# Attention and a PReLU MLP in one kernel: other order of MLP units, other first batch, and PReLU split over ACT, DVE and Pool

## The chip, the cores and the metric

One NeuronCore of a Trainium2 chip. The metric is device time of one execution in microseconds (us). The program runs on one core. Engines: PE (TensorE), ACT (ScalarE), DVE (VectorE), POOL (GpSimd), SP (DMA issue).

## The reference

```python
# q, k, v: (8, 12, 448, 64); w_in (768, 2048), w_out (2048, 768), alpha (2048)
q_n, k_n = rmsnorm(q, g_q), rmsnorm(k, g_k)
attn = softmax(q_n @ k_n.T / 8)            # per batch and head
x = (attn @ v) as (3584, 768)
h = x @ w_in
g = np.maximum(h, 0.0) + alpha * np.minimum(h, 0.0)      # PReLU, 0 <= alpha < 0.3
out = g @ w_out
```

## The kernel before: the parts that matter

Attention runs in steps ("gaps", numbered n) of two score tiles each. A pair of heads in both halves (index y, 24 of them) takes 3.5 gaps. Some gaps hold more: the softmax denominators (`den`, D), the product with v (`attv`, A), the transposes of the next q and k (`turn`, T). The MLP of a finished batch is cut into 16 "ups" (one 128-wide slice of h, index ft) and "downs" (one 128-token, 384-wide output), which are dealt out over the gaps to keep PE busy. A period is the ten or eleven gaps of one batch.

```python
psf = tile_pool(name="psf", bufs=2, space=PSUM)     # hT, op and spin share two buffers

def up(b, ft):
    hT = psf.tile([128, 512], FP32, name="hT", tag="mm")
    ...six matmuls...
    ah = ffn.tile([128, S], FP16, name="ah", tag="ah", bufs=3)
    nc.scalar.activation(out=ah, in_=hT[:, :S], func=AF.Copy, scale=alpha_sb[:, ft : ft + 1])
    nc.vector.tensor_max(out=gT[:, ft, ds((b & 1) * S, S)], in0=hT[:, :S], in1=ah)

def down(b0, t, oh):
    op = psf.tile([128, 512], FP32, name="op", tag="mm")
    for ft in range(NF):  nc.tensor.matmul(op, lhsT=gT[:, ft, ts(t, 128)], rhs=w_out_sb[...])
    ...DVE copy to osb, DMA out...

for y in range(G, NG):               # norm of the later q and k, each step in a gap of its own
    n = J * y / 2
    at(n - 12, load_qk, y)
    at(n - 6, square, y, nm)         # Pool
    after(n - 5, reduce, y, nm)      # DVE, 1.04 us each, two of them
    after(n - 4, root, y)            # ACT: Ln, Exp
    at(n - 3, scale, y, nm)          # Pool: qs
```

The softmax here doesn't subtract the row's maximum and nothing guards it: scores larger than these inputs give would overflow.

## Time and profile before

490.0 us (489.69 to 491.02, three runs).

| | before |
|---|---|
| span of the profiled run | 486.5 us |
| PE busy / idle | 448.4 / 38.1 us |
| first up, after its wait for xT (two of its matmuls ran at 51.92) | from 53.25 us |
| PE waits of hT for gT | 17.0 us, 30 waits |
| Pool busy | 166.7 us |

The prediction shows the lines behind this. The page gives for each engine its busy time; a wait is shown as who waited, for whom, the us in total, the number of waits, and the longest.

### The profile page before, as it was taken

The numbers are of one execution on the slowest core, as the hardware profiler recorded it, in microseconds if no ns is written. First come the engines' busy times: TensorE is split into PE (matmuls) and PEld (weight loads), VectorE is DVE, ScalarE is ACT, GpSimd is POOL, SyncE is SP. The second block draws the span as 40 slices with busy tenths as digits, with TensorE's granted clock in tenths as the row PEclk, the third lists the DMA queues.
The fourth block names the chain that finished last, engine by engine and source line by source line (L and its number), as shares of the span: only waits on it lengthen the run. The fifth ranks groups of instructions, "written<-read, shape, count | busy, mean of one in ns | idle before, by whom it ended". The sixth has DMA issues, their size and how long they took to land.

```text
span 486.5 us, 9510 instructions
## 1 busy us (share of the span) xinstructions
PE 448.4 (92%) x4072; PEld 234.3 (48%) x4072; DVE 216.7 (45%) x312; ACT 290.7 (60%) x399; POOL 166.7 (34%) x123
## 2 busy tenths in 40 slices
PE   6768799999999899999999899999999899999995
PEld 2334354544555444554555454554555454454563
DVE  1753545453552454544562444634643542334421
ACT  2688788666754667557765656666776475523300
POOL 2767574606504425405415244423435020000000
PEclk9599999999999999999999999999999999999999
DMA  7999996343605081333532280333511110120122
GB/s 210 158 248 244 239 197 117 71 109 87 134 23 124 20 165 51 91 98 85 96 74 74 70 166 5 105 80 97 100 34 34 34 34 0 34 66 0 34 65 66
DMA packets 32187, 45.46 MB, mean 93 GB/s; under 512 B 5008, under 2 KB 28560, under 8 KB 32144
## 3 DMA queue, kind: packets, MB, share of 16 engines
q1 hardware_dynamic: 19504, 31.67, 25.5%
q0 software_dynamic: 11776, 11.80, 15.3%
q10 hardware_dynamic: 864, 1.38, 1.0%
q8 instruction: 32, 0.52, 0.4%
q14 instruction: 11, 0.09, 0.1%
HBM read 45.62 MB, written 11.01 MB: 116 GB/s over the span
## 4 chain that ended last, share of the span: by engine, by line
PE 71%; DVE 13%; ACT 11%; DMA 2%; issue 2%; POOL 0%; DVEq 0%
PE op L266 31%; PE hT L249 20%; PE sc L189 6%; PE dn L212 6%; DVE ss L133 5%; DVE gT L258 5%; ACT ah L257 5%; PE av L212 5%; ACT expT L201 4%; PE tps L166 3%; DMA nat<-in_q_dram 2%; ACT rden L232 1%; DVE kT L176 1%; DVE qT L174 1%; ACT rden L227 1%
## 5 line engine op out<-in xcount | busy, mean ns | idle before, releaser
L201 ACT ACTIVATE expT<-sc,expb 128x896 f16<-128x896 f32 x168 | 160.2, 1003 | 48.7 <-PE sc L189 48.4
L249 PE MATMUL hT<-xT,w_in_sb 128*128 128x448 f16 x768 | 159.5, 352 | 17.9 <-DVE gT L258 17.0
L266 PE MATMUL op<-w_out_sb,gT 128*128 128x384 f16 x896 | 152.9, 326 | 0.2 <-DVE gT L258 0.2
L150 POOL TENSOR_TENSOR qs<-nat,rr 128x896 f16<-128x896 f32 x45 | 75.0, 1686 | 221.6 <-ACT rr L145 211.8
L257 ACT ACTIVATE ah<-hT,alpha_sb 128x448 f16<-128x448 f32 x128 | 81.1, 634 | 101.7 <-PE hT L249 100.7
L258 DVE TENSOR_TENSOR gT<-hT,ah 128x448 f16<-128x448 f32 x128 | 79.5, 624 | 104.3 <-ACT ah L257 104.2
L249 PEld LDWEIGHTS <-w_in_sb 128*128 128x128 f16 x768 | 72.3, 97 | 95.0 <-issue 35.4
L266 PEld LDWEIGHTS <-gT 128*128 128x128 f16 x896 | 85.0, 98 | 64.1 <-issue 10.5
L276 DVE COPY osb<-op 128x384 f32<-128x384 f32 x56 | 31.2, 558 | 112.1 <-PE op L266 112.1
L127 POOL TENSOR_TENSOR sq<-nat 128x896 f32<-128x896 f32 x44 | 72.9, 1676 | 3.0 <-DVE ss L133 3.0
L189 PE MATMUL sc<-qT,kT 64*64 64x448 f16 x672 | 50.2, 367 | 7.5 <-DVE kT L176 5.8
L133 DVE TENSOR_REDUCE ss<-sq 128x14 f32<-128x896 f32 x48 | 49.7, 1076 | 9.1 <-ACT sq L125 9.1
L240 DVE TENSOR_TENSOR xT<-av,rden 128x896 f16<-128x896 f32 x24 | 26.2, 1091 | 31.6 <-PE av L212 31.6
L212 PE MATMUL av<-expT,vt 64*64 64x448 f16 x672 | 36.0, 349 | 1.2 <-ACT rden L227 1.2
L212 PE MATMUL dn<-expT,ones 64*64 64x448 f16 x672 | 35.9, 349 | 0.0
L189 PEld LDWEIGHTS <-kT 64*64 64x64 f16 x672 | 13.4, 105 | 38.6 <-issue 30.2
L166 PE MATMUL tps<-ident,qs 128*128 128x128 f16 x336 | 24.0, 224 | 4.7 <-POOL qs L150 4.4
L212 PEld LDWEIGHTS <-vt 64*64 64x64 f16 x672 | 20.0, 107 | 13.5 <-issue 2.3
L166 PEld LDWEIGHTS <-qs 128*128 128x128 f16 x336 | 19.4, 100 | 13.5 <-issue 7.0
L212 PEld LDWEIGHTS <-ones 64*64 64x64 f16 x672 | 19.9, 107 | 11.8 <-issue 0.3
L227 ACT ACTIVATE rden<-dn 128x896 f32<-128x896 f32 x24 | 22.0, 916 | 4.8 <-PE dn L212 4.8
L232 ACT ACTIVATE rden<-rden 128x896 f32<-128x896 f32 x24 | 22.7, 947 | 0.3
(25 smaller groups left out, 97.3 us busy)
## 6 DMA issues: line engine op xcount, KB each, us to landing
out_dram<-osb SPq DMA_DIRECT2D x56, 192.0 KB, 2.7
nat<-in_q_dram SPq DMA_DIRECT2D x45, 224.0 KB, 3.8
nat<-in_k_dram SPq DMA_DIRECT2D x45, 224.0 KB, 5.0
vt<-in_v_dram POOLq DMA_DIRECT2D x16, 336.0 KB, 6.5
w_in_sb<-in_moe_w_in_dram POOLq DMA_DIRECT2D x4, 768.0 KB, 19.4
w_out_sb<-in_moe_w_out_dram POOLq DMA_DIRECT2D x4, 768.0 KB, 14.6
nat<-in_q_dram ACTq DMA_DIRECT2D x3, 224.0 KB, 6.9
nat<-in_k_dram ACTq DMA_DIRECT2D x3, 224.0 KB, 5.9
```

What stands on the lines that cost most here:

```text
L127: nc.gpsimd.tensor_mul(out=sqf, in0=src, in1=src)
L133: nc.vector.tensor_reduce(out=ss_t[y][:, "qk".index(nm)].rearrange("p h j -> p (h j)").unsqueeze(2), in_=sqs[y, nm], axis=AXIS_X, op=ALU.add,)
L150: eng.tensor_mul(out=t.rearrange("p j h d -> p h j d"), in0=nat[y, nm], in1=rr_t[y][:, "qk".index(nm)].unsqueeze(3).broadcast_to((128, 2, ...
L166: nc.tensor.transpose(tp[:, j, :], qs[y, nm][:, j].rearrange("p h d -> p (h d)"), ident)
L189: nc.tensor.matmul(out=sc[ds(64 * g, 64), par, :S], lhsT=kT[ds(64 * par, 64), g, j, :], rhs=qT[ds(64 * par, 64), g].rearrange("p j c -> p ...
L201: nc.scalar.activation(out=expT[y][:, j], in_=scs[y, j][:, :, :S], func=AF.Exp, scale=QK_SCALE, bias=expb[:, 0:1],)
L212: nc.tensor.matmul(out=acc[ds(64 * par, 64), g, :S], lhsT=weights(g, par, j), rhs=e[ds(64 * g, 64), j, par, :], start=(j == 0), stop=(j == ...
L249: nc.tensor.matmul(out=hT[:, :S], lhsT=w_in_sb[:, c, ts(ft, 128)], rhs=x[:, c, :], start=(c == 0), stop=(c == KM - 1),)
L257: nc.scalar.activation(out=ah, in_=hT[:, :S], func=AF.Copy, scale=alpha_sb[:, ft : ft + 1])
L258: nc.vector.tensor_max(out=gT[:, ft, ds((b & 1) * S, S)], in0=hT[:, :S], in1=ah)
L266: nc.tensor.matmul(out=op[:, :OH], lhsT=gT[:, ft, ts(t, 128)], rhs=w_out_sb[:, ft, ds(oh * OH, OH)], start=(ft == 0), stop=(ft == NF - 1),)
L276: nc.vector.tensor_copy(out=o[:, ds(oh * OH, OH)], in_=op[:, :OH])
```

## The change

Its intent: empty the PSUM buffer of an up faster (ACT and DVE read it side by side, Pool adds), put downs where DVE is busy with something else and reductions under downs, and start the first batch sooner. The diff, cut to its core:

```diff
@@ load_qk
-                (nc.scalar if y < G and g else nc.sync).dma_start(
+                (nc.scalar if y < 2 and g else nc.sync).dma_start(
@@ up
-        ah = ffn.tile([128, S], FP16, name="ah", tag="ah", bufs=3)
-        nc.scalar.activation(out=ah, in_=hT[:, :S], func=AF.Copy, scale=alpha_sb[:, ft : ft + 1])
-        nc.vector.tensor_max(out=gT[...], in0=hT[:, :S], in1=ah)
+        pos = ffn.tile([128, S], FP16, name="pos", tag="pos", bufs=4)
+        nc.scalar.activation(out=pos, in_=hT[:, :S], func=AF.Relu)
+        neg = ffn.tile([128, S], FP16, name="neg", tag="neg", bufs=4)
+        nc.vector.tensor_scalar(out=neg, in0=hT[:, :S], scalar1=0.0,
+            scalar2=alpha_sb[:, ft : ft + 1], op0=ALU.min, op1=ALU.mult)
+        nc.gpsimd.tensor_add(out=gT[...], in0=pos, in1=neg)
@@ down: jobs (the reductions) stand between its matmuls and its copy
+        for f, a in jobs:
+            f(*a)
@@ norm of later pairs
-        n = J * y / 2
-        at(n - 12, load_qk, y)   ... square n - 6, reduce n - 5, root n - 4, scale n - 3
+        n = turn_at[y - 1] if y < G + 2 else last(y - G) + 2
+        at(n - 8, load_qk, y)    ... square n - 2, reduce n (under the down of gap n), root and scale n + 1
@@ deal of units over gaps
-        ups and old downs merged evenly, then the new downs
+        in gaps with A or T: an old down first; else ups first; then the new downs
-        tail = len(new) if b == B - 1 else len(new) // 2
+        tail = len(new) if b == B - 1 else 2 + odd
@@ first batch
-    spin(32)                     +    spin(34)
-        after(1, reduce, 2, nm)  +        after(2, reduce, 2, nm)
-    after(2, root, 2)            +    roots[3] = 2     # root, scale after the exponentials
```

More of the change, by code (lines that the diff above doesn't have):

```diff
@@ L255, in up, with down @@
             )
-        ah = ffn.tile([128, S], FP16, name="ah", tag="ah", bufs=3)
-        nc.scalar.activation(out=ah, in_=hT[:, :S], func=AF.Copy, scale=alpha_sb[:, ft : ft + 1])
-        nc.vector.tensor_max(out=gT[:, ft, ds((b & 1) * S, S)], in0=hT[:, :S], in1=ah)
+        pos = ffn.tile([128, S], FP16, name="pos", tag="pos", bufs=4)
+        nc.scalar.activation(out=pos, in_=hT[:, :S], func=AF.Relu)
+        neg = ffn.tile([128, S], FP16, name="neg", tag="neg", bufs=4)
+        nc.vector.tensor_scalar(
+            out=neg, in0=hT[:, :S], scalar1=0.0, scalar2=alpha_sb[:, ft : ft + 1],
+            op0=ALU.min, op1=ALU.mult,
+        )
+        nc.gpsimd.tensor_add(out=gT[:, ft, ds((b & 1) * S, S)], in0=pos, in1=neg)
     osb = {}
-    def down(b0, t, oh):
+    def down(b0, t, oh, jobs=()):
         op = psf.tile([128, 512], FP32, name="op", tag="mm")
@@ L300 @@
     avs = {last(y) + 2: y for y in range(NG)}
-    prep, post = {}, {}
+    prep, post, roots = {}, {}, {}
     def at(n, f, *a):
@@ L307, in after @@
         post.setdefault(max(int(n), 0), []).append((f, a))
+    turn_at = [J * y // 2 - 1 for y in range(NG)]
+    turns = {n: y for y, n in enumerate(turn_at) if y}
+    jobs = {}
     for y in range(G, NG):
-        n = J * y / 2
-        at(n - 12, load_qk, y)
+        n = turn_at[y - 1] if y < G + 2 else last(y - G) + 2
+        at(n - 8, load_qk, y)
         for nm in "qk":
-            at(n - 6, square, y, nm)
-            after(n - 5, reduce, y, nm)
-        after(n - 4, root, y)
-        for nm in "qk":
-            at(n - 3, scale, y, nm)
+            at(n - 2, square, y, nm)
+            if y < G + 2:
+                after(n, reduce, y, nm)
+            else:
+                jobs.setdefault(n, []).append((reduce, (y, nm)))
+        roots[n + 1] = y
     for b in range(1, B):
         at(J * G * b / 2 - 4, load_v, b)
-    turns = {J * y // 2 - 1: y for y in range(1, NG)}
     UP, DOWN = 1.13, 2.6
-    def merge(ups, downs):
-        res, done = [], 0
-        for n, u in enumerate(ups):
-            while done < len(downs) and done * len(ups) <= n * len(downs):
-                res.append(downs[done])
-                done += 1
-            res.append(u)
-        return res + downs[done:]
     periods, carry = [], []
@@ L341 @@
         ]
-        tail = len(new) if b == B - 1 else len(new) // 2
-        periods.append(merge(ups, carry) + new[:tail])
+        tail = len(new) if b == B - 1 else 2 + odd
+        periods.append((ups, carry, new[:tail]))
         carry = new[tail:]
@@ L353 @@
         hi = last(G * b + 2 * G - 1) + 2
-        mlp = sum(u[0] for u in periods[b])
+        ups, old, new = (list(u) for u in periods[b])
+        mlp = sum(u[0] for u in ups + old + new)
         per = (mlp + sum(cost(n) for n in range(lo, hi))) / (hi - lo)
-        n, clock, done = lo, cost(lo), 0.0
-        for u in periods[b]:
-            while n < hi - 1 and clock + 0.5 * u[0] > per * (n - lo + 1):
-                n += 1
-                clock += cost(n)
-            gaps[n].append(u[1:])
-            clock += u[0]
-    rest = [u[1:] for u in periods[B - 1]]
+        clock = 0.0
+        for n in range(lo, hi):
+            clock += cost(n)
+            free = n in avs or n in turns
+            while ups or old or new:
+                if old and (free or not ups):
+                    u = old.pop(0)
+                elif ups:
+                    u = ups.pop(0)
+                else:
+                    u = new.pop(0)
+                gaps[n].append(u[1:])
+                clock += u[0]
+                free = False
+                ahead = 0.5 * (UP if ups else DOWN)
+                if n < hi - 1 and clock + ahead > per * (n - lo + 1):
+                    break
+    ups, old, new = periods[B - 1]
+    rest = []
+    for n, u in enumerate(ups):
+        if n % 3 == 0 and old:
+            rest.append(old.pop(0)[1:])
+        rest.append(u[1:])
+    rest += [u[1:] for u in old + new]
     load_qk(0)
@@ L373 @@
     nc.sync.dma_start(out=alpha_sb, in_=moe_alpha.rearrange("(t p) -> p t", p=128))
-    spin(32)
+    spin(34)
     for nm in "qk":
@@ L395 @@
         after(0, scale, 1, nm)
-        after(1, reduce, 2, nm)
-    after(2, root, 2)
-    for nm in "qk":
-        after(2, scale, 2, nm)
+        after(2, reduce, 2, nm)
+    roots[3] = 2
     for n in range(NB + 2):
@@ L406 @@
             score(*t)
-        late = []
         if n in dens:
@@ L413 @@
         wait = plain and gaps[n] and gaps[n][0][0] is up
+        late = []
         for t in tiles[:1] if wait else tiles:
@@ L416 @@
         if wait:
-            late = [(soft, t) for t in tiles[1:]]
+            late = [(1, soft, t) for t in tiles[1:]]
         if n in dens:
             log(dens[n])
-            late = [(invert, (dens[n],))]
+            late = [(2, invert, (dens[n],))]
+        if n in roots:
+            y = roots[n]
+            root(y)
+            for nm in "qk":
+                scale(y, nm)
         if n in turns:
             turn(turns[n])
+        done = 0
         for f, a in gaps[n]:
-            f(*a)
-            if f is up and late:
-                for g, c in late:
-                    g(*c)
-                late = []
-        for g, c in late:
+            if f is down:
+                down(*a, jobs.pop(n, ()))
+            else:
+                f(*a)
+                done += 1
+                if late and done == late[0][0]:
+                    for _, g, c in late:
+                        g(*c)
+                    late = []
+        for _, g, c in late:
             g(*c)
         if n < first:
-            spin(1 if not plain else 4)
-        for f, a in post.get(n, ()):
+            spin(4 if plain else 1)
+        for f, a in jobs.pop(n, []) + post.get(n, []):
             f(*a)
```

## The prediction

> **What bounds the kernel now.** I read the page's busy shares first, then the waits of the PE alone, then tables by window, then the PE and DVE timelines of one period in the middle (182 to 241 us).
>
> ```profile
> PE 448.4 (92%) x4072; PEld 234.3 (48%) x4072; DVE 216.7 (45%) x312; ACT 290.7 (60%) x399; POOL 166.7 (34%) x123
> ...
> PE hT L249 <- DVE gT L258: 17.0, 30, 1.4
> PE sc L189 <- DVE kT L176: 5.8, 4, 2.0
> PE tps L166 <- POOL qs L150: 4.4, 1, 4.4
> ```
>
> PE is the bound: 448.4 of 486.5 us. All that can be won is its idle 38 us. Of this, 17.0 us in 30 waits is an up-projection (hT) waiting until the PSUM buffer of the unit two before is emptied: hT, op and spin share two buffers, and a unit is free when ACT (ah) and then DVE (gT) have read it. The rest lies in the first 53 us and at the very end.
>
> ```profile
> 0.00:20.00 20.00, 12.86 (x66) 5.72 (x66) 7.48 (x12) 8.12 (x13) 7.92 (x15) 0.80 0.83 185
> 20.00:40.00 20.00, 14.67 (x193) 7.07 (x189) 10.56 (x11) 16.87 (x23) 16.31 (x14) 0.95 1.13 231
> 40.00:60.00 20.00, 15.86 (x183) 8.16 (x183) 10.01 (x13) 16.67 (x21) 11.69 (x9) 1.00 1.17 244
> ...
> 182.00:240.00 58.00, 55.38 (x522) 29.16 (x524) 29.31 (x42) 37.46 (x55) 22.78 (x16) 1.00 0.35 81
> ```
>
> The columns are PE, PEld, DVE, ACT and POOL busy us. From 20 to 53 us there is attention alone (spin matmuls pad PE), and ACT with its exponentials is the fullest engine, some 16.8 of 20 us. Later PE is busy 55.4 of 58 us: a period loses only 2.6 us.
>
> ```profile
> 218.88 2.07 DVE L133 TENSOR_REDUCE ss<-sq 128x14 f32<-128x896 f32 x2
> 220.87 1.26 DVE L258 TENSOR_TENSOR gT<-hT,ah 128x448 f16<-128x448 f32 x2
> ...
> 221.53 1.29 PE L249 MATMUL hT<-xT,w_in_sb 128*128 128x448 f16 x6 [1.02 <-DVE gT L258]
> 216.34 1.30 PE L249 MATMUL hT<-xT,w_in_sb 128*128 128x448 f16 x6 [0.25 <-DVE gT L258]
> ```
>
> This is what a wait consists of. A third up in a row waits 0.25 us by the chain ACT 0.63 + DVE 0.62 + hand-overs, less the 1.15 us of the up between. Where the two 1.04 us reductions stand in DVE's queue ahead of gT, it is 1.02 us (1.36 with other work beside). So the large waits come from where the reductions are put.
>
> **What the Trainium skill says.** (1) "PSUM — Partial Sum Buffer", section "PSUM bank collisions raise a hardware error": two engines may not touch one bank and partition quadrant together, ScalarE read beside VectorE read included, so software orders them. Relu "beside" alpha*min is therefore not beside it. In the built order of the changed program each DVE neg waits for ACT alone and not for PE: it follows pos on the same hT. The trace of before can't show this, as its gT needed ah anyway. (2) "ScalarE: Activation LUTs", section "What ACT_TABLE_LOAD costs": an ACTIVATE takes 186 ns + 0.833 ns per element, and 93 ns more per pointer operand. For 448 elements with one pointer that is 652 ns; the trace's ah takes 634, so it agrees. Relu has no pointer: estimate 634 - 93 = 541 ns. (3) "GPSIMD Engine Reference", section 3.1: a two-input add of 2048 fp32 took 4497 ns, 2.2 ns per element. The trace is faster, 1686 ns for 896 (1.88), so I use the trace. (4) "VectorE: DVE Perf Modes", the perf-mode tier table: two-input and one-input operations with an fp32 PSUM source both run at 1x. So neg should take what gT took, 0.62 us.
>
> **The change part by part.**
>
> PReLU. The chain that frees a PSUM buffer goes from 0.63 + 0.62 to an estimated 0.54 + 0.62 us. The back-to-back wait falls from 0.25 to about 0.16. ACT saves 128 x 0.09 = 12 us of busy time, which is hidden later on. Pool gets 128 adds at 448 x 1.88 ns = 0.84 us (estimate), 108 us: 166.7 + 108 = 274 us, 56% of the span, not a bound. But gT is now ready a Pool add later, and Pool is a queue in order.
>
> Reductions and order of units. The reductions of a pair of heads move to the gap after the attention-value product, between the down-projection's matmuls (2.65 us on PE) and its copy, and there they are hidden. A down goes first where DVE is busy with xT or with qT and kT. This should remove the eight or so 1.02 to 1.36 us waits. But in gaps that have no down they still stand in DVE's queue, now ahead of qT and kT of the next gap, whose scores then wait.
>
> I walked through both kinds of period with the trace's durations (scores 0.41, den or av 1.43, transposes 0.79, up 1.17, down 2.65, exp 0.89, log 0.82, root 0.55, reduction 1.04, qT and kT together 1.2, qs 1.68).
> - Even period: two gaps of three ups after den 0.24 each; five ups in a row 0.4; up, up, down at the end of the period 0.35 for the buffer. Then the down's weights ft 14 and 15 come from the last two ups, whose adds stand on Pool behind two qs of 3.35 us that wait for root. Gap-local: root ends at 2.8, qs at 6.1, the adds at 7.0 and 7.9. The down starts at 3.95 and wants ft 14 at 3.95 + 14 x 0.164 = 6.25, so it stalls 0.8 + 0.75, some 1.5 us. Sum 2.75.
> - Odd period: small waits 0.75 in sum; at its end three ups with no down, reductions behind them, then two ups beside the turn: kT late by 0.75, buffer 0.35, and the same Pool stall 1.5. Sum 3.35.
> - Before, a pair of periods lost 4.57 us (0.24, 1.36, 0.34, 1.02, 0.25, 1.02, 0.34 in the PE timeline). After: 6.1.
> - First period of the MLP: reductions at the end of gaps without a down, kT late three times, 3.8 us against 3.2. Last period with attention 0.75, as no qs is left. The tail of ups and downs 1.5 against 1.8.
> Sum after: 3.8 + 3 x 3.35 + 2 x 2.75 + 0.75 + 1.5 = 21.6 us, against 17.0 + 0.8 (the first up's wait for xT) = 17.8 before. The middle loses 3.8 us.
>
> First batch. Before, ACT itself issues the loads of the third pair, which wait for earlier transfers: the issue at 8.68 keeps it from squaring until 9.33 us, while q of the first pair had landed near 4.9. After, q is squared near 5.0 and k at its landing (8.65), not at 10.2. The k chain (reduction, Ln, Exp, DVE scale, transposes) then gives first scores some 1.5 us earlier, and near 2.0 with PE's pause shortened from 4.4 to about 2 us, since the granted clock at 12 to 18 us was 0.50 and may now stay up. From then on ACT leads. Reductions behind qT and kT and root behind the exponentials remove the 2.04 us wait for kT and some 0.95 us of ACT idle, while one new ACT wait for reductions (0.9) comes at the fourth gap. Gap by gap the lead goes 2.3, 2.5, 3.6, 3.1. The head wins 3.1 us.
>
> Sum: 490.0 + 3.8 - 3.1 = 490.7. The walk leaves no slack for hand-overs that happen to overlap, and its stalls are upper sides, while a saved wait is sure where the reductions lie under a down. I take 1.7 us off for this and predict 489.0.
>
> **Rivals.**
> (a) ACT and DVE do run side by side, or the Pool stall is absent because the last adds get ahead of qs. Then the middle loses only the small waits: some 21.6 - 7.5 (five stalls of 1.5) = 14 us, with the head 490 - 3.7 - 3.1 = 483; without the late kT as well 480. For it: Pool is idle over 60% before. Against it: the built order has qs ahead of those adds, and neg behind pos.
> (b) Pool becomes a moving bound: an add takes 1.2 us or more (the skill's two-input rate plus a fixed part), so pos and neg, four buffers each, run out, and ACT waits for Pool. Each period then loses 2 to 3 us more: 505. For it: rough Pool times. Against it: 16 adds and three pairs of sq and qs take 13.4 + 20.2 = 34 us of a 58 us period.
> (c) The head's gain is hidden: the weights or the loads of later pairs set the first up. Then 493. Against it: w_in is issued at 21.3 and lands within some 20 us, before 53.
>
> **Range and chances.** The base case is 489; (a) in part draws to 481, (c) and longer stalls to 496. Range 481 to 496. Faster by over 2% needs under 480.2, all of (a): 0.12. Slower by over 2% needs (b), over 499.8: 0.07. Within 2%: 0.81.
>
> **What would show it.** Right: first exponential near 15.3 us rather than 17.6; first up near 50; pos near 540 ns, neg near 620 with its idle time ended by ACT pos; Pool adds near 0.84 us; the 1.0 to 1.4 us waits of hT gone, with waits of hT near 0.2; new waits of PE (its weight loads) for Pool gT at the ends of periods, about 1.5 us each, and of scores for kT of about 0.75. PE idle in the middle 2.5 to 3.5 us a period. Wrong: neg running at the same time as pos; no waits for Pool gT; many ACT waits for Pool; a first exponential no earlier than before.

## The result, and the profile after

495.5 us (494.99 to 496.0, four runs) against 490.5 (489.69 to 491.06). The ratio is 1.0103, 95% interval 1.0082 to 1.0124: 1% slower. A second run of the changed kernel later gave 1.0115.

The page's busy line and the waits of PE alone, changed kernel:

```profile
PE 453.5 (92%) x4074; PEld 234.8 (48%) x4074; DVE 224.5 (45%) x312; ACT 277.4 (56%) x399; POOL 296.1 (60%) x251
...
PE hT L249 <- DVE neg L260: 8.5, 25, 1.1
PE sc L189 <- DVE kT L176: 7.4, 10, 1.3
PE op L272 <- POOL gT L264: 7.4, 10, 0.8
PE sc L189 <- ACT expT L201: 3.9, 7, 1.0
```

The waits of hT were halved, 17.0 to 8.5 us. A new wait of the downs for Pool, 7.4 us, and more waits of scores came in their place. The three groups of PReLU (busy us, mean ns; then idle time ahead of them and what ended it):

```profile
L264 POOL TENSOR_TENSOR gT<-pos,neg 128x448 f16<-128x448 f16 x128 | 130.1, 1030 | 105.9 <-DVE neg L260 102.7
L260 DVE TENSOR_SCALAR neg<-hT,alpha_sb 128x448 f16<-128x448 f32 x128 | 86.9, 684 | 120.9 <-ACT pos L258 120.9
L258 ACT ACTIVATE pos<-hT 128x448 f16<-128x448 f32 x128 | 68.7, 543 | 110.7 <-PE hT L249 104.8
```

All of neg's 120.9 us of idle time was ended by ACT's pos: the two readers of one hT run one after the other, 0.54 + 0.68 us, where before it was 0.63 + 0.62. Next to nothing was gained on the chain, 1.23 against 1.26 us. The windows by stage, to be read as those in the prediction:

```profile
0.00:20.00 20.00, 15.77 (x76) 6.36 (x80) 9.52 (x14) 10.03 (x15) 10.20 (x17) 0.85 0.96 200
...
182.00:240.00 58.00, 54.73 (x530) 28.53 (x529) 27.36 (x38) 34.43 (x51) 37.20 (x32) 1.00 0.30 67
```

The middle is a little emptier on PE (54.73 of 58 us, 55.38 before). To see where the 7.0 us of span arise, I compared the start of the logarithm of each pair of heads (ACT, line 227, one per pair) in both timelines:

| pair y | before | after | after - before |
|---|---|---|---|
| 2 (end of the head) | 49.50 | 47.29 | -2.21 |
| 8 | 149.59 | 148.51 | -1.08 |
| 14 | 261.37 | 263.81 | +2.44 |
| 20 | 373.13 | 379.10 | +5.97 |
| 23 | 427.55 | 431.92 | +4.37 |
| end of span | 486.5 | 493.5 | +7.0 |

The head wins 2.2 us. Two periods (y = 8 to 14) take 115.30 us in place of 111.78, so 1.8 us are lost in each. From y = 23 to the end 2.6 us more pass; one down (2.65 us on PE) has moved from the periods to the end, and what it costs there was saved earlier. From the end of the head to the end of the span the changed kernel therefore loses 7.0 + 2.2 = 9.2 us; this is the middle of the prediction.

The end of period 1 shows the main loss. Lines of the timeline of the changed kernel (start, us, engine, operation; in brackets the idle time before, and what ended it):

```profile
137.88 0.96 ACT L258 ACTIVATE pos<-hT 128x448 f16<-128x448 f32 x2
138.05 3.33 POOL L150 TENSOR_TENSOR qs<-nat,rr 128x896 f16<-128x896 f32 x2 [1.56 <-ACT rr L145]
138.44 1.28 DVE L260 TENSOR_SCALAR neg<-hT,alpha_sb 128x448 f16<-128x448 f32 x2
...
139.18 2.44 PE L272 MATMUL op<-w_out_sb,gT 128*128 128x384 f16 x14 [0.25 <-DVE neg L260]
...
141.34 2.01 POOL L264 TENSOR_TENSOR gT<-pos,neg 128x448 f16<-128x448 f16 x2
...
142.43 0.34 PE L272 MATMUL op<-w_out_sb,gT 128*128 128x384 f16 x1 [0.82 <-POOL gT L264]
...
143.41 2.77 PE L272 MATMUL op<-w_out_sb,gT 128*128 128x384 f16 x16 [0.65 <-POOL gT L264]
```

pos and neg of the last two ups are done at 139.7. Pool is in two qs until 141.4 and adds them only then. The down does 14 matmuls and stops for ft 14 and again for ft 15. Its 16th matmul starts 4.23 us after its first, where 15 x 0.1625 = 2.44 us is normal (16 matmuls take 2.60 us when nothing stops them): 1.79 us lost. The recorded waits are 1.47 us, less than that, since the record of a matmul that stands alone (0.34 us) is longer than its place in a full stream (0.16). The same stall appears at 202, 257, 317 and 373 us.

### The profile page after: what moved, and what is told of

The parts are those of the page before. It is cut to its first block, busy times and chain, and to the rows that moved or that the text cites. A ratio compares the mean times of both kernels' runs of the same rounds, so it can differ in the third digit from the quotient of the medians.

```text
span 493.5 us, 9659 instructions
## 1 busy us (share of the span) xinstructions
PE 453.5 (92%) x4074; PEld 234.8 (48%) x4074; DVE 224.5 (45%) x312; ACT 277.4 (56%) x399; POOL 296.1 (60%) x251
## 3 DMA queue, kind: packets, MB, share of 16 engines
q0 software_dynamic: 11776, 11.80, 15.3%
## 4 chain that ended last, share of the span: by engine, by line
PE 61%; POOL 13%; ACT 9%; DVE 8%; issue 6%; DMA 1%; POOLq 0%; SPq 0%; ACTq 0%; DVEq 0%
PE op L272 26%; PE hT L249 17%; PE sc L189 6%; PE av L212 6%; POOL qs L150 5%; PE dn L212 4%; DVE neg L260 4%; POOL sq L127 4%; ACT pos L258 4%; POOL gT L264 3%; ACT expT L201 3%; DVE ss L133 3%; PE tps L166 2%; DMA nat<-in_k_dram 1%; POOL vt L102 1%
## 5 line engine op out<-in xcount | busy, mean ns | idle before, releaser
L264 POOL TENSOR_TENSOR gT<-pos,neg 128x448 f16<-128x448 f16 x128 | 130.1, 1030 | 105.9 <-DVE neg L260 102.7
L272 PE MATMUL op<-w_out_sb,gT 128*128 128x384 f16 x896 | 155.3, 327 | 9.0 <-POOL gT L264 7.4
L260 DVE TENSOR_SCALAR neg<-hT,alpha_sb 128x448 f16<-128x448 f32 x128 | 86.9, 684 | 120.9 <-ACT pos L258 120.9
L258 ACT ACTIVATE pos<-hT 128x448 f16<-128x448 f32 x128 | 68.7, 543 | 110.7 <-PE hT L249 104.8
L272 PEld LDWEIGHTS <-gT 128*128 128x128 f16 x896 | 84.9, 98 | 74.3 <-POOL gT L264 11.2
L150 POOL TENSOR_TENSOR qs<-nat,rr 128x896 f16<-128x896 f32 x45 | 75.0, 1688 | 58.0 <-ACT rr L145 46.9
L284 DVE COPY osb<-op 128x384 f32<-128x384 f32 x56 | 31.1, 555 | 95.6 <-PE op L272 95.6
L189 PE MATMUL sc<-qT,kT 64*64 64x448 f16 x672 | 51.7, 370 | 11.4 <-DVE kT L176 7.4
```

Of the source, the lines that this page charges most:

```text
L150: eng.tensor_mul(out=t.rearrange("p j h d -> p h j d"), in0=nat[y, nm], in1=rr_t[y][:, "qk".index(nm)].unsqueeze(3).broadcast_to((128, 2, ...
L189: nc.tensor.matmul(out=sc[ds(64 * g, 64), par, :S], lhsT=kT[ds(64 * par, 64), g, j, :], rhs=qT[ds(64 * par, 64), g].rearrange("p j c -> p ...
L258: nc.scalar.activation(out=pos, in_=hT[:, :S], func=AF.Relu)
L260: nc.vector.tensor_scalar(out=neg, in0=hT[:, :S], scalar1=0.0, scalar2=alpha_sb[:, ft : ft + 1], op0=ALU.min, op1=ALU.mult,)
L264: nc.gpsimd.tensor_add(out=gT[:, ft, ds((b & 1) * S, S)], in0=pos, in1=neg)
L272: nc.tensor.matmul(out=op[:, :OH], lhsT=gT[:, ft, ts(t, 128)], rhs=w_out_sb[:, ft, ds(oh * OH, OH)], start=(ft == 0), stop=(ft == NF - 1),)
```

## The experiments

All were correct. Each was timed with three rounds against the kernel before on the same chip; the kernel before had medians of 488.54 (first four), 489.58 (next four) and 489.66 us (last two), so the differences, and not the times, are to be compared across chips.

| run | median us | against before, us | ratio (95%) |
|---|---|---|---|
| changed kernel | 495.48 | +5.0 | 1.0103 (1.0082 to 1.0124) |
| r1_old_prelu | 482.35 | -6.2 | 0.9878 (0.9849 to 0.9907) |
| r2_only_prelu | 494.54 | +6.0 | 1.0123 (1.0098 to 1.0148) |
| r3_head_only | 486.47 | -2.1 | 0.9951 (0.9920 to 0.9982) |
| r4_last_two | 484.19 | -4.4 | 0.9909 (0.9883 to 0.9934) |
| r5_add_on_dve | 490.25 | +0.7 | 1.0014 (0.9980 to 1.0049) |
| r6_old_prelu_late_red | 479.25 | -10.3 | 0.9792 (0.9759 to 0.9825) |
| r7_eight_bufs | 492.24 | +2.7 | 1.0057 (1.0023 to 1.0091) |
| r8_late_red | 486.64 | -2.9 | 0.9941 (0.9902 to 0.9981) |
| r9_early_red | 477.87 | -11.8 | 0.9766 (0.9747 to 0.9785) |
| r10_after_again | 495.01 | +5.4 | 1.0115 (1.0091 to 1.0138) |

**r1_old_prelu: everything but the PReLU.**

```diff
 changed kernel
-        pos = ...Relu;  neg = ...min, mult;  nc.gpsimd.tensor_add(out=gT[...], in0=pos, in1=neg)
+        ah = ...Copy, scale=alpha;  nc.vector.tensor_max(out=gT[...], in0=hT[:, :S], in1=ah)
```

> The changed kernel with the PReLU of before (ACT copy times alpha, DVE max); gap order and first batch as changed. Theory (the loss sits in the Pool add: five stalls of 1.8 us at the ends of periods 1 to 5, counted from the first down's start to its 16th matmul, a buffer stall of some 1.5 us near 83 us, and a DVE part of 0.68 instead of 0.62 us): 485 us, that is 10 below the changed kernel, and no PE wait for Pool gT. Rival (the new order of units and the reductions placed behind ups without a down cost it): 494 us, as the PReLU would not matter.

6.2 us below before and 11.2 below the changed kernel (-6.2 against +5.0), and no wait for Pool gT is left among PE's. The rival falls: order and first batch are good by themselves. In r1's profiled run 0.84 us comes from an early landing of k; see the head in the part on the prediction. PE's waits in this run:

```profile
PE hT L249 <- DVE gT L259: 6.5, 25, 0.3
PE sc L189 <- DVE kT L176: 4.5, 5, 1.3
PE sc L189 <- ACT expT L201: 3.5, 7, 0.5
PE sc L189 <- ACT ah L258: 2.9, 5, 0.8
```

The longest wait of hT is 0.3 us, where it was 1.4 before: the reductions are out of its way.

r1 and the changed kernel have the same order, so their logarithms can be compared pair by pair. The lead of r1 grows in steps and is nearly flat in between:

| pair y at which the lead grows | step, us | what is there in the changed kernel |
|---|---|---|
| 8, 14, 20 | 1.87 each | stall of the down, odd periods |
| 11, 17 | 1.78, 1.77 | stall of the down, even periods |
| 5 | 1.56 | ACT waits 2.19 us for Pool gT at 81 us |
| 10, 16 | 0.89, 0.88 | ACT waits 1.70 and 1.69 us for Pool gT at 185 and 301 us |
| 3 to 23, in sum | 12.2 | five stalls 9.2 and three buffer waits 3.3, less 0.3 of drift |

**r2_only_prelu: the PReLU alone.** The same edit the other way round, on the kernel before.

> The kernel before with only the PReLU of the change. If the PReLU is dear by itself, as a longer chain with a Pool step: 498 us or more. Theory: it is dear only where a down follows the last ups and qs stands ahead of their adds on Pool; in the order of before the qs are issued gaps later, so the adds are done in time and the kernel takes 491 to 493 us (0.03 us more in each short wait, a few waits of ACT for the four buffers).

6.0 us slower. The theory had 491 to 493 us, some 1 to 3 above the 490 of the kernel before, and the rival 498 or more: neither size is right. Between pairs 4 and 5 the distance to the kernel before changes from -0.9 to +5.1 us, and by only 0.5 us in all the pairs after that, though ACT waits 17.4 us in this run for Pool's work (14.4 of them recorded as for qs): nearly all of that is hidden. So the PReLU is not dear by itself, but in one place. The timeline there, and then the kernel before at the same place:

```profile
80.75 3.33 POOL L150 TENSOR_TENSOR qs<-nat,rr 128x896 f16<-128x896 f32 x2
84.04 3.31 POOL L127 TENSOR_TENSOR sq<-nat 128x896 f32<-128x896 f32 x2
87.32 2.01 POOL L263 TENSOR_TENSOR gT<-pos,neg 128x448 f16<-128x448 f16 x2
...
88.39 0.34 PE L271 MATMUL op<-w_out_sb,gT 128*128 128x384 f16 x1 [1.96 <-POOL gT L263]
89.38 0.50 PE L271 MATMUL op<-w_out_sb,gT 128*128 128x384 f16 x1 [0.65 <-POOL gT L263]
...
92.17 4.48 PE L271 MATMUL op<-w_out_sb,gT 128*128 128x384 f16 x16
```

```profile
84.83 2.77 PE L266 MATMUL op<-w_out_sb,gT 128*128 128x384 f16 x16
87.54 0.57 PE L189 MATMUL sc<-qT,kT 64*64 64x448 f16 x8
```

It is the same mechanism in one place: two adds behind 6.6 us of qs and sq. And two things cost time. The first down takes 5.83 us to the next scores (2.71 in the kernel before at the same place), so 3.1 us are the stall. Then the granted clock has fallen: the columns of the windows are as before, the clock is third from the end.

```profile
88.00:90.00 2.00, 0.95 (x6) 0.39 (x10) 0.08 (x1) 0.00 (x0) 1.33 (x2) 0.70 0.02 3
90.00:92.00 2.00, 2.00 (x21) 1.30 (x14) 2.00 (x3) 1.55 (x2) 0.00 (x0) 0.50 0.00 0
```

At half clock the stretch from these scores to the next ones takes 6.77 us in place of 3.99, which is the other 2.8 us. That the pause of PE brought the clock down is read from the order in this one trace, and no run tests it.

**r3_head_only: the first batch alone.** The kernel before with the loads of the third pair off ACT's queue, `spin(34)`, and reductions and roots of pairs 2 to 4 placed as in the change.

> The kernel before with only the first batch reordered (loads of the third pair off ACT's queue, reductions behind qT and kT, root behind the exponentials, for the pairs 0 to 4). Theory: the first up starts 2.2 us earlier, as in the changed kernel, and nothing takes it back: 488.3 us. Rival (the gain in the head is hidden by a later wait): 490.3.

2.1 us faster by the medians, 2.4 by the ratio. In its profiled run the lead of 1.9 us at pair 2 stands unchanged at pair 23: nothing takes it back.

**r4_last_two: Pool adds for 14 of 16 slices only.**

```diff
 changed kernel, up()
+        if ft >= NF - 2:
+            ...ah and tensor_max of the kernel before...
+            return
         pos = ...
```

> The changed kernel, but the last two ups of each batch (ft 14 and 15) with the PReLU of before, so only 16 of 128 adds leave Pool. Theory (the five stalls of the first down behind qs are the main loss): 495.5 - 5 x 1.8 = 486.5 us and no PE wait for Pool gT at ft 14 and 15. Rival (Pool's load as a whole, or the chain of ACT and DVE, costs it): 494 us, an eighth of the difference.

9.4 us below the changed kernel with only 16 of 128 adds taken from Pool. The rival, that Pool's load or the chain costs it, would have given one eighth. Pair by pair r4 gains five steps of 1.78 to 1.82 us where the stalls were, 9.0 in sum, and a sixth of 1.53 us near 83 us, as it also takes the first of the three buffer waits away; the other two stay. In this run qs still stands on Pool at that place, and the down runs through (the row goes on past the 16 matmuls of one down):

```profile
137.17 4.06 PE L277 MATMUL op<-w_out_sb,gT 128*128 128x384 f16 x24 [0.28 <-DVE gT L260]
...
136.02 3.33 POOL L150 TENSOR_TENSOR qs<-nat,rr 128x896 f16<-128x896 f32 x2 [1.56 <-ACT rr L145]
```

**r5_add_on_dve: the add on DVE.**

```diff
-        nc.gpsimd.tensor_add(out=gT[...], in0=pos, in1=neg)
+        nc.vector.tensor_add(out=gT[...], in0=pos, in1=neg)
```

> The changed kernel with the sum of pos and neg on DVE instead of Pool; Relu on ACT and alpha*min on DVE stay. Theory (Pool's queue delays gT; the split itself costs only 0.03 us per short wait): no PE wait for gT longer than 0.3 us, and 1 to 2 us above the kernel with the whole PReLU of before, that is about 5 us below the kernel before. Rival (three instructions in place of two are what costs): above the kernel before, as DVE now has one more instruction on the chain.

+0.7 us (the interval of the ratio takes in 1), where I expected about -5: a miss. There is no wait for Pool's gT, but hT now waits up to 0.7 us. The add on DVE took 560 ns in the mean, and 128 of them stand in the queue that also frees hT:

```profile
L264 DVE TENSOR_TENSOR gT<-pos,neg 128x448 f16<-128x448 f16 x128 | 71.7, 560 | 4.4
...
PE hT L249 <- DVE neg L260: 11.1, 31, 0.7
PE sc L189 <- DVE kT L176: 9.9, 10, 1.3
```

The mean hides two kinds. By tile, the 128 adds last 391 ns at the least, 393 in the middle and 1577 at the most. The 93 during which Pool ran nothing took 391 to 394 ns each; the 32 that met a square (sq) or a qs there took 600 to 1577, and 3 that met only the issue of a load took 392 or 393. The views by tile, of Pool and of DVE:

```profile
L264 DVE TENSOR_TENSOR gT<-pos,neg x128: 391/393/1577, 52.6 to 463.1; 128x448 f16<-128x448 f16 x128
103.34 3.46 POOL L127 TENSOR_TENSOR sq<-nat 128x896 f32<-128x896 f32 x2
103.69 1.57 DVE L264 TENSOR_TENSOR gT<-pos,neg 128x448 f16<-128x448 f16 x1
```

So the add left Pool's queue, but was still slow whenever one of Pool's long operations ran. neg beside it (670 to 686 ns) and the gT of the kernel before (614 to 626) show nothing of the kind. This is read from the trace; no run without Pool's work at those places tests it. The split into three instructions is dear on DVE too: the PReLU of two instructions is 6.9 us better in the same order (r1).

**r7_eight_bufs: pos and neg with eight buffers.**

```diff
-  pos ... bufs=4    neg ... bufs=4
+  pos ... bufs=8    neg ... bufs=8
```

> The changed kernel with eight buffers in place of four for pos and neg. Theory (Pool's backlog reaches ACT only near 78 to 84 us, where ACT waits for Pool gT 5.6 us in three waits and scores follow by 1.5 us): at most 2 us below the changed kernel, the stalls of the downs unchanged. Rival (the backlog is general): 5 us or more.

2.3 us below the changed kernel (2.7 against r10), about the 2 us expected. The place was read wrongly: the three waits are not all near 78 to 84 us, but at 81, 185 and 301 us. At all three Pool has a pair of squares (3.3 us) and the issue of a load of v (1.35 us) ahead of the adds. Pair by pair r7 gains 1.59, 0.86 and 0.85 us there, 3.3 in sum, and nothing elsewhere. ACT's waits for Pool go from 5.6 to 0.4 us, and the waits of hT of 1.1 us go. The stalls of the downs stay: PE's waits for Pool gT read 7.4 us in ten here too. Changed kernel (sum of the waits, and one of the three in the timeline), then this run:

```profile
ACT pos L258 <- POOL gT L264: 5.6, 3, 2.2
185.22 0.54 ACT L258 ACTIVATE pos<-hT 128x448 f16<-128x448 f32 x1 [1.70 <-POOL gT L264]
```

```profile
ACT pos L258 <- POOL gT L264: 0.4, 2, 0.2
```

**r8_late_red: reductions, root and qs of pairs 10, 16, 22 two gaps later.**

```diff
 changed kernel, norm of later pairs
         n = turn_at[y - 1] if y < G + 2 else last(y - G) + 2
+        if y in (10, 16, 22):
+            n += 2
```

> The changed kernel, PReLU with Pool kept, with the reductions, root and qs of the pairs 10, 16 and 22 two gaps later. So at the end of the odd periods qs stands behind the adds of the last two ups and not ahead of them. Theory: the stalls for Pool gT of periods 1, 3 and 5 go (3 x 1.8 us), and the kT wait with them (3 x 0.8): 7 to 8 us below the changed kernel, 2 to 3 below the kernel before; those of periods 2 and 4 stay. Rival (the adds are late by their own load on Pool, not by qs): stalls stay in all five, 2 to 3 us gained.

2.9 us below before, 7.9 below the changed kernel, as expected. PReLU and the number of adds are the same. The whole preparation of three pairs (loads, squares, reductions, root, qs) comes two gaps later, so the order on Pool is not all that changes. The stalls fall from five to two:

```profile
PE op L272 <- POOL gT L264: 3.0, 4, 0.8
PE sc L189 <- DVE kT L176: 5.8, 7, 1.3
```

How much of the gain is the stalls? r6, below, makes the same shift without adds on Pool. Pair by pair it gains 1.05 us on r1 at each of y = 8, 14 and 20; r8 gains 2.86 us on the changed kernel at each. The difference, 1.81 us each or 5.4 in sum, is one stall each (by the medians, across chips, the sum is 3.8). So it is the place of qs ahead of the adds, and not the load of the adds.

**r6_old_prelu_late_red and r9_early_red: towards a version that beats both.** r6 is r1 with the edit of r8. r9 is r6 with one more:

```diff
+        if y in (5, 6, 7):
+            n -= 1
```

> The changed kernel with the PReLU of before, and the reductions of the pairs 10, 16 and 22 (the ones that stand behind three ups in a gap without a down) two gaps later, under a down. Theory: this takes away kT late by 0.55 to 0.8 and a buffer wait of 0.25 to 0.3 with their refill, three times: some 3 us below r1_old_prelu, 9 us below the kernel before. Rival (the scores' wait for kT hides another wait just behind it): the same as r1_old_prelu, 6 us below.

> r6_old_prelu_late_red with the reductions of the pairs 5, 6 and 7 one gap earlier, so that they stand ahead of the attention-value product and not ahead of the next qT and kT. Theory: the three waits of scores for kT between 57 and 89 us (0.8, 0.55, 0.4 us in the changed kernel) and their followers go: 2 us below r6_old_prelu_late_red, 12 below the kernel before. Rival (xT behind the reductions becomes the wait): no gain, 10 below the kernel before.

r6 came out 10.3 us below before, 4.1 below r1 by the differences. r9 came out 11.8 below, the expected 12, and 1.5 below r6; across chips, that last step is about as small as the noise, but in the traces it lies where it was expected: r9's lead over r6 grows by 1.96 us between pairs 2 and 4. r9 is the best kernel, 477.87 us. Its PE waits:

```profile
PE hT L249 <- DVE gT L259: 6.2, 24, 0.3
PE sc L189 <- DVE kT L176: 4.0, 4, 1.3
PE sc L189 <- ACT expT L201: 2.4, 5, 0.5
```

The four kT waits that are left all lie in the head (before 50 us); hT waits only the short 0.3 us of a third up in a row.

**r10_after_again: the changed kernel beside r9.**

> The changed kernel itself once more, on the chip and in the rounds of r9_early_red, so that the two are compared directly: 1.0% above the kernel before, as in its first run, by both theories; r9_early_red then 16 to 17 us below it.

495.01 against 477.87 us on one chip in the same rounds, 17.1 us apart.

## Why the prediction was right or wrong

489.0 was predicted, 481 to 496 as range, within 2% with a chance of 0.81. Measured were 495.5 us and +1.0%: within 2% and just inside the range, but on the other side of 490 from the point. The steps:

- **ACT and DVE do not read hT side by side: right.** All of neg's idle time ends with pos. pos took 543 ns (541 predicted).
- **The Pool stall at the ends of periods 1 to 5, through qs ahead of the last two adds: right in place, number and recorded size.** 10 waits in five pairs, 7.4 us in sum, 1.5 each predicted and recorded. r4, and r8 beside r6, show its cause.
- **The new order of units: right in size.** Without its 7.5 us of stalls the walk gives 14.1 us against 17.8, a gain of 3.7 in the middle. r1, which has the order without the Pool adds, gains 3.35 there in its trace.
- **Durations: two were too short.** The Pool add was scaled in proportion, 0.84 us, and took 1.03. neg was taken as equal to gT, 0.62, and took 0.68; the short wait of hT became 0.28 and not 0.16 us, of which neg explains 0.06. It mattered little: r1's 25 waits of hT sum to 6.5 us, those of r7 with the new PReLU to 6.9.
- **The sum of the middle: 3.8 us predicted, 9.2 found. This is the step that failed in size.** Two terms make up 5.0 of the missing 5.4 us. A stall costs some 1.8 us of PE's time and not its recorded 1.5: 9.2 in place of 7.5 (table in r1). And four buffers did run out: ACT waited for Pool three times, which costs 3.3 us in the traces (r7; 2.3 to 2.7 by the medians). This I had named as rival (b) and put aside by comparing Pool's busy time with the period. Pool is busy only 60%, but its work comes in blocks of 3.3 us. The order's missing 0.35 us is the rest.
- **The head: 3.1 us predicted, 2.2 found.** The start was right: the first exponential is at 15.38 us (15.3 predicted, 17.64 before), q is squared at 5.06 and k at 8.70. The lead predicted from there, 3.1, was 2.66 at the exponentials ahead of pair 0's logarithm and 2.21 at pair 2. Between the two the transposes wait 0.51 us for Pool's qs at 41.19, whose root now comes later, and ACT then waits 0.77 us for scores; the kernel before does not wait there. The clock did not stay up, as I had hoped: it was granted 0.50 between 14 and 20 us. But that cost nothing at pair 2. r1, with the clock at 1.00 there, and r5 have the same head and are at -3.05 and -2.91; they squared k at 7.84 and 7.99 us, and this 0.86 and 0.71 us is all of their lead over the changed kernel (0.84 and 0.70). r3, r4 and r10 fit this within 0.02 us, so the head of a run shifts with the landing of k; r6 to r9 lose 0.3 to 0.5 us more ahead of pair 2, which was not traced.
- **The 1.7 us taken off at the end: wrong in direction.** I read my walk as an upper side. It was a lower one, as every unexpected size made a wait longer.
- Rival (a) fell with neg's waits and the 7.4 us of waits for Pool, rival (c) with r3. Rival (b) came true in three places.

That the result lies inside the range, by half a us, is partly luck. The range ended at 496 for rival (c) and longer stalls. The stalls were longer by only 0.3 us each and (c) did not come, but part of (b), which the range left out, took its place.

Where did the expected gain of the change go? Order and first batch together are worth 6.2 us (r1), of which the first batch is 2.1 to 2.4 (r3). The new PReLU costs 11.2 us on top by the medians, 12.2 in the traces between pairs 2 and 23: 9.2 in five stalls of downs and 3.3 in three waits for buffers (r4 takes away 9.0 of the first and 1.5 of the second, r7 the 3.3).

Left open: why the DVE add of r5 is slow beside Pool's long operations, whether PE's pause brought the clock down in r2, and why neg takes 0.06 us longer than gT did.

## What to carry to other kernels

Before work is moved to an idle engine, look at what stands ahead of it in that engine's queue and who needs its result next: here an engine that was 34% busy, in blocks of 3.3 us, held up 1 us adds by 1.6 us (at 141 us) and, in r2, by 3.2. The split across two engines that read the same PSUM tile bought no overlap; look at what the second reader waits for in the built program. And a mean can hide two kinds of an operation (r5): ask for its least and greatest time. And judge a bundle of edits part by part: here two parts gained 6 us, the third lost 11.

## What the Trainium skill lacked or had wrong

- "GPSIMD Engine Reference", section 3.1, gives a two-input add at one size only, 4497 ns for 2048 fp32 elements (2.2 ns per element). The runs show 1688 ns for a two-input multiply of 896 fp32 elements (1.88 per element) and 1030 ns for the add of 448 fp16 elements (2.3 per element). The page names a dispatch cost but gives no figure for it; if both lay on one line, which they need not as the types differ, it would be some 370 ns (estimate from these two).
- "TensorE: Matmul & The Clock Gate", Part 1, says the clock falls after an idle window of about 3.4 us. In r2_only_prelu PE paused 1.96 us, ran one matmul (88.39 to 88.73 us) and paused 0.65 us, under 3 us in all, and the granted clock was 0.50 from about 88.8 to 95.6 us (estimate from its means over 1 us). The five pairs of pauses of some 0.82 and 0.65 us in the changed kernel left it at 1.00 (read in windows around all five).
- None of the pages on VectorE has the difference between one- and two-input DVE operations out of PSUM: at 128x448 the tensor_scalar with a pointer operand took 684 ns, the tensor_tensor 624.
